# Transposing the experts' rows by small DMAs and 32x32 blocks on VectorE instead of on TensorE

## The chip, the cores and the metric

The kernel runs on one core of a Trainium2 chip. The metric is device time in microseconds of one execution, the median of several runs.

## The reference

Two stages follow each other. A recurrent attention over r, k, v (batch 4, 8 heads, 768 steps, head size 48) gives 3072 rows x of 384 numbers. Each row is then routed to two of eight experts:

```
logits = x @ w_gate;  noisy = logits + log1p(exp(x @ w_noise)) * noise
top2 = the two largest of noisy;  top2_w = softmax over these two
for e in range(8), for k in range(2):
    mask = top2[:, k] == e
    h = maximum(x[mask] @ w1[e], 0)              # 384 -> 1024
    out[mask] += top2_w[mask, k] * (h @ w2[e])   # 1024 -> 384
```

## The kernel before

The attention part and the routing end at about 230 us and are not touched. After them comes a sequence `seq` of chunks (e, ci). Every expert has room for 832 of its rows, held as seven tiles: six of 128 rows and a tail of 64. Expert 0 has three chunks. Experts 1 to 7 have two: chunk (e, 0) holds the tiles 0, 1, 2 (384 rows), chunk (e, 1) the tiles 3, 4, 5 and the tail (448 rows).

Each pass of the loop `for s in range(2, len(seq))` works on one chunk and prepares later ones. Order on every engine is the order in which the program issues instructions; there is no scheduler.

- `xgather` (GpSimd) gathers the rows of the chunk two ahead from `xd` in DRAM, one indirect DMA per tile, into `xg` [128, 392] (384 numbers and 8 gate weights).
- `xT` brings the next chunk's rows into the layout with features on partitions: per tile three TensorE transposes into PSUM (`ptm`, L760), a ScalarE copy to `xh` (L761), a VectorE subtraction for the remainder `xl` (L762; numbers are split into a high and a low part so that three fast matmuls stand for one exact one), and a small copy `GT` of the gate weight (L763). It is a generator: two of its tiles are issued during phase 1, one behind each of the first tiles of phase 2.
- `p1` (phase 1, L781): for eight blocks f of 128 hidden units, nine matmuls into one of three buffers `ph`, then ScalarE's Relu (L783) and VectorE's remainder (L785) into `hb` and, for the tail's 64 columns, `ht`.
- `p2` (phase 2, L815, for the tail L806 and L808): for each tile 24 matmuls (tail: 16) into `pym`, then ScalarE's copy `ot` (L819).
- `emit_out` multiplies by the gate and adds the earlier expert's contribution `pv` (VectorE, L830) and scatters the rows (GpSimd, L834); `pgather` (L742) fetches `pv` for the next expert.
- `w_split` and `wstep` load the next expert's weights: a unit is one DMA of SyncE into one of three staging buffers `stg` (L273), three steps later ScalarE's copy `w0h` or `w1h` (L277), one step later VectorE's remainder (L279). The three units of w1 are taken up in chunk (e, 0), the four of w2 in chunk (e, 1).

Of the kernel before, what the change touches and what calls it, by code (L numbers as in the profile page):

```python
# [9 lines left out]
F32 = mybir.dt.float32  # L10
F32R = mybir.dt.float32r
# [3 lines left out]
AF = mybir.ActivationFunctionType  # L15
# [17 lines left out]
WARM1 = 2  # L33
WARM3 = 1
NLD = 4
XT_AT_0 = 4
XT_AT = 4
LREP = 6
# [4 lines left out]
def kernel(  # L43
# [14 lines left out]
    nc = tc.nc  # L58
    B, H, S, D = r.shape
    N, E = noise.shape  # L60
    DM = H * D
# [4 lines left out]
    ND = DM // 128  # L66
# [3 lines left out]
    NM = 6  # L70
# [3 lines left out]
    WMAX = 3 * 128 + TAIL  # L74
# [4 lines left out]
    NJ = NM + 1  # L79
    XW = DM + E  # L80
# [8 lines left out]
    psum = ctx.enter_context(tc.tile_pool(name="psum", bufs=1, space=bass.MemoryType.PSUM))  # L89
# [3 lines left out]
    moe = stack.enter_context(tc.tile_pool(name="moe", bufs=2, side="left", reuse_waits="tile"))  # L93
# [54 lines left out]
    ident = const.tile([128, 128], F32, name="ident")  # L148
# [33 lines left out]
    for src, store, pw, nm in ((kd[0], kT, pwk, "kT"), (rd[0], rT, pwr, "rT")):  # L182
        pt = psum.tile([128, NP, 128], F32, name="pt0", tag="pa", bufs=3)
# [76 lines left out]
    def w_split(e):  # L260
        W[e] = {}
        units = []

        def unit(mat, c0, c1, src):
            def f():
                if mat not in W[e]:
                    sh = [128, ND, FF] if mat == 0 else [128, NF, DM]
                    W[e][mat] = [wpool[e % 2].tile(sh, F32R, name=f"w{mat}{x}{e % 2}", bufs=1) for x in "hl"]
                hi, lo = (t[:, c0:c1, :] for t in W[e][mat])
                t = stg.tile([128, 1024], F32, name="stg")  # L270
                n = hi.shape[1] * hi.shape[2]
                tv = t[:, :n].rearrange("p (a b) -> p a b", b=hi.shape[2])
                nc.sync.dma_start(tv, src)  # L273
                yield
                yield
                yield
                nc.scalar.activation(hi, tv, AF.Copy)  # L277
                yield
                nc.vector.tensor_sub(lo, tv, hi.bitcast(F32))  # L279
                yield  # L280
            return f()

        for c in range(ND):
            units.append(unit(0, c, c + 1, w1[e, c * 128:(c + 1) * 128, :].rearrange("(c p) f -> p c f", p=128)))
        for c in range(0, NF, 2):
            units.append(unit(1, c, c + 2, w2[e, c * 128:(c + 2) * 128, :].rearrange("(c p) d -> p c d", p=128)))
        return units
# [3 lines left out]
    def wstep():  # L291
        for un in list(wrun):
            if next(un, 0) == 0:
                wrun.remove(un)
        if wq and len(wrun) < 3:
            un = wq.pop(0)
            next(un)
            wrun.append(un)
# [423 lines left out]
    def tw(t):  # L722
        return TAIL if t == NM else 128

    XG, XH, HH, PV, OT, scat_of = {}, {}, {}, {}, {}, {}
    def chunks(e):
        return CHUNKS1 if e else CHUNKS0

    def xgather(e, ci, early_=False):
        for t in chunks(e)[ci]:  # L730
            n = tw(t)
            xg = moe.tile([128, XW], F32, name="xg", bufs=6)
            nc.gpsimd.indirect_dma_start(  # L733
                out=xg[:n], out_offset=None, in_=xd[:GROUPS[GEARLY - 1][1] * 128] if early_ else xd,
                in_offset=bass.IndirectOffsetOnAxis(ap=GR[:n, e * NJ + t:e * NJ + t + 1], axis=0))
            XG[e, t] = xg

    def pgather(e):
        for t in range(NM + 1):
# [4 lines left out]
                in_offset=bass.IndirectOffsetOnAxis(ap=GA[:n, e * NJ + t:e * NJ + t + 1], axis=0))  # L744
            PV[e, t] = pv

    def xT(e, ci):
        xh = moe.tile([128, ND, WMAX], F32R, name="xh")
        xl = moe.tile([128, ND, WMAX], F32R, name="xl")
        XH[e, ci] = (xh, xl)  # L750
        o = 0
        for t in chunks(e)[ci]:
            n = tw(t)
            if (e, t) == (0, NM):
                pt = psum.tile([128, ND, 128], F32, name="ptm", tag=f"py{np2[0] % 2}")
                np2[0] += 1
            else:
                pt = psum.tile([128, ND, 128], F32, name="ptm", tag="pt", bufs=2)
            for d in range(ND):
                nc.tensor.transpose(pt[:, d, :n], XG[e, t][:n, d * 128:(d + 1) * 128], ident[:n, :n])  # L760
            nc.scalar.activation(xh[:, :, o:o + n], pt[:, :, :n], AF.Copy)  # L761
            nc.vector.tensor_sub(xl[:, :, o:o + n], pt[:, :, :n], xh[:, :, o:o + n].bitcast(F32))  # L762
            nc.scalar.activation(GT[:n, e * NJ + t:e * NJ + t + 1], XG[e, t][:n, DM + e:DM + e + 1], AF.Copy)  # L763
            o += n
            yield

    def p1(e, ci):
        w_ = sum(tw(t) for t in chunks(e)[ci])
        xh, xl = XH[e, ci]
        wh, wl = W[e][0]  # L770
        wb = w_ // 128 * 128
        hb = moe.tile([128, NF, 2, 3 * 128], F32R, name="hb", bufs=1)
        ht = moe.tile([128, NF, 2, TAIL], F32R, name="ht", bufs=1) if w_ > wb else None
        HH[e, ci] = (hb, ht)
        parts = [(hb[:, :, :, :wb], 0, wb)] + ([(ht, wb, w_)] if w_ > wb else [])
        for f in range(NF):
            fs = slice(f * 128, (f + 1) * 128)
            ph = psum.tile([128, WMAX], F32, name="ph", tag="pa", bufs=3)
            q = [(a, x, d) for d in range(ND) for a, x in ((wh, xh), (wh, xl), (wl, xh))]
            for j, (a, x, d) in enumerate(q):  # L780
                nc.tensor.matmul(ph[:, :w_], a[:, d, fs], x[:, d, :w_], start=(j == 0), stop=(j == len(q) - 1))  # L781
            for h_, a, b in parts:
                nc.scalar.activation(h_[:, f, 0, :], ph[:, a:b], AF.Relu)  # L783
            for h_, a, b in parts:
                nc.vector.scalar_tensor_tensor(h_[:, f, 1, :], ph[:, a:b], 0.0, h_[:, f, 0, :].bitcast(F32),  # L785
                                               op0=ALU.max, op1=ALU.subtract)
            yield

    np2 = [0]

    def p2(e, ci):
        hb, ht = HH[e, ci]
        wh, wl = W[e][1]
        offs = {t: 128 * j for j, t in enumerate(chunks(e)[ci])}

        ts = chunks(e)[ci]
        for t in ts if (e, ci) != seq[-1] else ts[-1:] + ts[:-1]:
            n, o = tw(t), offs[t]
            py = psum.tile([128, DM], F32, name="pym", tag=f"py{np2[0] % 2}")
            np2[0] += 1  # L800
            ot = moe.tile([128, DM], F32, name="ot", bufs=NOT)
            OT[e, t] = ot
            hs = slice(o, o + n)
            if n == 64:
                for f in range(NF):
                    nc.tensor.matmul(py, ht[:, f].rearrange("p a b -> p (a b)"), wh[:, f, :], start=(f == 0), stop=(f == NF - 1),  # L806
                                     skip_group_check=True)
                    nc.tensor.matmul(py[:n], ht[:, f, 0, :], wl[:, f, :], start=False, stop=(f == NF - 1),  # L808
                                     skip_group_check=True)
                nc.scalar.activation(ot[:n], py[64:], AF.Copy)  # L810
                nc.vector.tensor_add(ot[:n], py[:n], ot[:n])
            else:
                q = [(a, x, f) for f in range(NF) for a, x in ((0, wh), (0, wl), (1, wh))]
                for j, (a, x, f) in enumerate(q):
                    nc.tensor.matmul(py, hb[:, f, a, hs], x[:, f, :], start=(j == 0), stop=(j == len(q) - 1))  # L815
                if (e, ci) == seq[-1]:
                    OT[e, t] = py
                else:
                    nc.scalar.activation(ot, py, AF.Copy)  # L819
            yield t  # L820
# [158 lines left out]
    for s in range(2, len(seq)):  # L979
        e, ci = seq[s]  # L980
        end = s + 1 == len(seq)
        if e and ci == 0:
            nxt = w_split(e + 1) if e + 1 < E else []
            wq.extend(nxt[:ND])
        elif e:
            wq.extend(nxt[ND:])
        xt = xT(*seq[s + 1]) if not end else iter(())
        for j, _ in enumerate(p1(e, ci)):
            while hold:
                emit_out(*hold.pop(0))  # L990
            if XT_AT <= j < XT_AT + 2:
                next(xt, None)
            wstep()
        if s + 2 < len(seq):
            xgather(*seq[s + 2])

        for t in p2(e, ci):
            next(xt, None)
            wstep()
            hold.append((e, t))  # L1000
            while len(hold) > (0 if end else 1):
                emit_out(*hold.pop(0))
        if ci == len(chunks(e)) - 1 and not end:
            while hold:
                emit_out(*hold.pop(0))
            pgather(e + 1)
# [77 lines left out]
```

## Time and profile before

| | us |
|---|---|
| median of 3 runs | 679.81 (676.81 to 680.94) |
| the profiled execution, its own time | 673.61 |
| its span in the trace | 671.8 |
| TensorE busy | 633.3 |
| VectorE busy | 344.7 |
| ScalarE busy | 278.2 |
| GpSimd busy | 251.6 |
| mean granted TensorE clock | 0.968 of full speed |

The busy times are those of one execution, taken by the hardware profiler. In the rows of the profile, PE is TensorE, PEld its weight loads, DVE VectorE, ACT ScalarE, POOL GpSimd, and SPq the queue of SyncE, which issues DMAs. A row of the timeline has start and length in us, engine, line, operation, tile written and tiles read, shape, count, and in brackets the idle time before it and who ended it. A row of the table of groups ends with busy time, mean ns of one, and idle time before.

### The profile page before, as it was taken

What the parts mean: (1) busy time and instruction counts of PE and PEld (TensorE: products, weight loads), DVE (VectorE), ACT (ScalarE), POOL (GpSimd) and SP (SyncE); (2) the same over time, 40 slices, a digit from 0 to 9 for tenths busy, and PEclk for the clock granted to TensorE, in tenths of its full rate; (3) what the DMA queues carried; (4) which work ended last, traced back from release to release, by engine and by line L of the source; (5) the groups of instructions that cost most, each with busy time, mean ns of one, the idle gap of its engine ahead of it and who ended that gap; (6) DMA issues with size and microseconds to landing.
All of it is one profiled execution on the core that took longest, in us unless ns stands there. A gap on an engine that the chain in (4) does not pass through costs nothing.

```text
span 671.8 us, 11840 instructions
## 1 busy us (share of the span) xinstructions
PE 633.3 (94%) x4420; PEld 605.5 (90%) x4421; DVE 344.7 (51%) x837; ACT 278.2 (41%) x809; POOL 251.6 (37%) x318
## 2 busy tenths in 40 slices
PE   7998789897999799999999999999999999999993
PEld 4998788887889799999999999999999999999993
DVE  7675996678547673452525425344362534424230
ACT  4897556655332253252423414244242524422220
POOL 7465323524120353621741442264154236315111
PEclk9999888978699999999999999999999999999997
DMA  7999445734120572532524254262424426302001
GB/s 126 211 220 224 121 115 132 186 86 112 60 91 1 166 251 71 172 119 89 172 86 145 67 164 140 68 184 71 148 89 131 139 68 184 101 27 84 36 4 35
DMA packets 111445, 78.87 MB, mean 117 GB/s; under 512 B 86721, under 2 KB 101441, under 8 KB 111378
## 3 DMA queue, kind: packets, MB, share of 16 engines
q1 hardware_dynamic: 101442, 49.19, 28.5%
q0 software_dynamic: 9936, 28.83, 13.5%
q8 instruction: 37, 0.61, 0.4%
q14 instruction: 30, 0.25, 0.1%
HBM read 59.03 MB, written 19.76 MB: 117 GB/s over the span
## 4 chain that ended last, share of the span: by engine, by line
PE 68%; DVE 2%; ACT 0%; issue 0%; POOL 0%; POOLq 0%
PE ph L781 31%; PE pym L815 30%; PE ptm L760 3%; PE pym L808 2%; PE pym L806 2%; DVE r_oa L579 0%; DVE xl L762 0%; DVE hb L785 0%; PE py L388 0%; PE pl L418 0%; DVE r_ob L586 0%; DVE r_ob L582 0%; ACT xh L761 0%; POOL out_dram L834 0%; PE py L380 0%
## 5 line engine op out<-in xcount | busy, mean ns | idle before, releaser
L815 PE MATMUL pym<-w1h,hb 128*128 128x384 f32 x768 | 204.2, 339 | 0.0
L781 PE MATMUL ph<-xh,w0h 128*128 128x384 f32 (+3 forms) x408 | 141.6, 347 | 1.2 <-ACT xh L761 1.2
L815 PEld LDWEIGHTS pym<-w1h,hb 128*128 128x128 f32 x768 | 139.5, 188 | 0.6
L781 PE MATMUL ph<-xl,w0h 128*128 128x384 f32 (+3 forms) x408 | 138.8, 340 | 0.3 <-DVE xl L762 0.2
L781 PE MATMUL ph<-xh,w0l 128*128 128x384 f32 (+3 forms) x408 | 138.8, 340 | 0.0
L834 POOL DMA_INDIRECT out_dram<-ot,TK x56 | 57.1, 1020 | 216.1 <-DVE ot L830 198.1
L815 PE MATMUL pym<-w1l,hb 128*128 128x384 f32 x384 | 129.2, 336 | 0.0
L785 DVE SCALAR_TENSOR_TENSOR hb<-ph,hb 128x384 fp32r<-128x384 f32 (+1 forms) x136 | 72.3, 532 | 110.2 <-ACT ht L783 70.3
L783 ACT ACTIVATE hb<-ph 128x384 fp32r<-128x384 f32 (+1 forms) x136 | 64.2, 472 | 113.7 <-PE ph L781 111.7
L819 ACT ACTIVATE ot<-pym 128x384 f32<-128x384 f32 x45 | 22.1, 491 | 160.5 <-PE pym L815 160.5
L733 POOL DMA_INDIRECT xg<-xd,GR x56 | 55.1, 984 | 76.7 <-DVE ti L614 37.3
L781 PEld LDWEIGHTS ph<-xh,w0h 128*128 128x128 f32 x408 | 76.7, 188 | 4.1 <-ACT xh L761 1.5
L781 PEld LDWEIGHTS ph<-xl,w0h 128*128 128x128 f32 x408 | 76.7, 188 | 3.2 <-DVE xl L762 0.8
L781 PEld LDWEIGHTS ph<-xh,w0l 128*128 128x128 f32 x408 | 76.6, 188 | 2.6
L815 PEld LDWEIGHTS pym<-w1l,hb 128*128 128x128 f32 x384 | 72.2, 188 | 0.1
L762 DVE TENSOR_TENSOR xl<-ptm,xh 128x384 fp32r<-128x384 f32 (+1 forms) x56 | 29.0, 524 | 81.3 <-ACT xh L761 81.3
L388 PE MATMUL py<-vt,am 128*128 128x96 f32 x384 | 63.3, 296 | 5.6 <-DVE am L346 5.2
L742 POOL DMA_INDIRECT pv<-out_dram,GA x49 | 55.7, 1138 | 28.2 <-issue 13.7
L388 PEld LDWEIGHTS py<-vt,am 128*128 128x128 f32 x384 | 55.8, 211 | 6.5 <-DVE am L346 6.4
L304 POOL TENSOR_TENSOR kd<-kt,tabk 128x384 f32<-128x384 f32 x23 | 24.9, 1083 | 86.0 <-PE pwarm L356 72.5
L319 ACT ACTIVATE cv<-vt,c 128x48 f32<-128x48 f32 x192 | 45.9, 321 | 5.0 <-DVE c L316 4.7
L346 DVE TENSOR_TENSOR am<-pa,mneg 128x512 int32<-128x512 int32 x48 | 30.9, 684 | 15.8 <-PE pa L338 15.8
(196 smaller groups left out, 868.9 us busy)
## 6 DMA issues: line engine op xcount, KB each, us to landing
stg<-in_moe_w_dram SPq DMA_DIRECT2D x24, 512.0 KB, 4.2
stg<-in_moe_w_dram SPq DMA_DIRECT2D x32, 384.0 KB, 3.6
rd<-in_r_dram SPq DMA_DIRECT2D x24, 192.0 KB, 3.9
vt<-in_v_dram SPq DMA_DIRECT2D x24, 192.0 KB, 3.7
xd<-x SPq DMA_DIRECT2D x24, 192.0 KB, 2.3
out_dram<-zrow SPq DMA_DIRECT2D x16, 288.0 KB, 3.6
kt<-in_k_dram SPq DMA_DIRECT2D x23, 192.0 KB, 3.8
xg<-xd,GR POOLq DMA_INDIRECT x56, 3.2
```

The costliest lines, as they stand in the source:

```text
L304: (eng or nc.gpsimd).tensor_mul(kd[i % 3][:, :, :D], kt[i], tabk[:, :, :D])
L319: nc.scalar.activation(cv[:, h, :], vt[i][:, h, :], AF.Copy, scale=c8[:, h, :])
L346: nc.vector.tensor_tensor(am[:, s].bitcast(I32), pa[s].bitcast(I32), mneg.to_broadcast([128, NP, 128]), op=ALU.bitwise_and)
L388: nc.tensor.matmul(o2, AM[i][:, s, p, :], vt[i][:, h, None, :].to_broadcast([128, 2, D]), start=not c and h == 0, stop=h == H - 1, skip_gr ...
L733: nc.gpsimd.indirect_dma_start(out=xg[:n], out_offset=None, in_=xd[:GROUPS[GEARLY - 1][1] * 128] if early_ else xd, in_offset=bass.Indirec ...
L742: nc.gpsimd.indirect_dma_start(out=pv[:n], out_offset=None, in_=out, in_offset=bass.IndirectOffsetOnAxis(ap=GA[:n, e * NJ + t:e * NJ + t + ...
L762: nc.vector.tensor_sub(xl[:, :, o:o + n], pt[:, :, :n], xh[:, :, o:o + n].bitcast(F32))
L781: nc.tensor.matmul(ph[:, :w_], a[:, d, fs], x[:, d, :w_], start=(j == 0), stop=(j == len(q) - 1))
L783: nc.scalar.activation(h_[:, f, 0, :], ph[:, a:b], AF.Relu)
L785: nc.vector.scalar_tensor_tensor(h_[:, f, 1, :], ph[:, a:b], 0.0, h_[:, f, 0, :].bitcast(F32), op0=ALU.max, op1=ALU.subtract)
L815: nc.tensor.matmul(py, hb[:, f, a, hs], x[:, f, :], start=(j == 0), stop=(j == len(q) - 1))
L834: st = nc.gpsimd.indirect_dma_start(out=out, out_offset=bass.IndirectOffsetOnAxis(ap=TK[:n, q:q + 1], axis=0), in_=ot[:n], in_offset=None, ...
```

## The change

For experts 2 to 7 (`ESP = 2`) the rows are gathered into one buffer `xgt` with place for a chunk's four tiles. At the start of the pass for chunk s, `spread` issues 16 SyncE DMAs that copy the rows of chunk s+1 inside SBUF to `xq`: 32 rows and 96 features each, so that every 32x32 block lies on the right partitions. In phase 2 of that pass, one VectorE instruction per tile transposes all blocks of the tile in place, and `xh` and `xl` are made from `xq`. Both `xgt` and `xq` have one buffer. Partition 32a + j now holds feature 96a + 32c + j for c = 0, 1, 2, so w1 of these experts is loaded with its rows in the same order, in four DMAs of 32 rows for each of its three parts. `xh` and `xl` have a new layout for all experts, [128, 14, 3, 32] instead of [128, 3, 448], and phase 1 reads them in runs of 32 columns. The gate copies move to the end of the pass before.

The diff, cut to its core:

```diff
+ESP = 2
...
-                nc.sync.dma_start(tv, src)
+                if mat or e < ESP:
+                    nc.sync.dma_start(tv, src)
+                else:
+                    for a in range(4):
+                        nc.sync.dma_start(tv[32 * a:32 * a + 32, 0, :], src[a])
...
-            units.append(unit(0, c, c + 1, w1[e, c * 128:(c + 1) * 128, :].rearrange("(c p) f -> p c f", p=128)))
+            units.append(unit(0, c, c + 1, w1[e].rearrange("(a c j) f -> c a j f", a=4, j=32)[c] if e >= ESP else
+                              w1[e, c * 128:(c + 1) * 128, :].rearrange("(c p) f -> p c f", p=128)))
...
     def xgather(e, ci, early_=False):
-        for t in chunks(e)[ci]:
+        if e >= ESP:
+            XGT[e, ci] = late[0].tile([128, 4, XW], F32, name="xgt", bufs=1)
+        for j, t in enumerate(chunks(e)[ci]):
             n = tw(t)
-            xg = moe.tile([128, XW], F32, name="xg", bufs=6)
+            xg = XGT[e, ci][:, j] if e >= ESP else moe.tile([128, XW], F32, name="xg", bufs=6)
...
+    def spread(e, ci):
+
+        xq = late[0].tile([128, WMAX // 32, 96], F32, name="xq", bufs=1)
+        XQ[e, ci] = xq
+        w_ = sum(tw(t) for t in chunks(e)[ci]) // 32
+        for q in range(4):
+            m = (w_ - q + 3) // 4
+            for a in range(4):
+                nc.sync.dma_start(xq[32 * a:32 * a + 32, q:w_:4],
+                                  XGT[e, ci][32 * q:32 * q + 32, :m, a * 96:(a + 1) * 96])
+
+    def gate(e, ci, t):
+        q, n = e * NJ + t, tw(t)
+        nc.scalar.activation(GT[:n, q:q + 1], XG[e, t][:n, DM + e:DM + e + 1], AF.Copy)
...
+            if e >= ESP:
+                v = XQ[e, ci][:, g].rearrange("p t (c j) -> p t c j", j=32)
+                nc.vector.transpose(v, v)
...
-            nc.scalar.activation(xh[:, :, o:o + n], pt[:, :, :n], AF.Copy)
-            nc.vector.tensor_sub(xl[:, :, o:o + n], pt[:, :, :n], xh[:, :, o:o + n].bitcast(F32))
-            nc.scalar.activation(GT[:n, e * NJ + t:e * NJ + t + 1], XG[e, t][:n, DM + e:DM + e + 1], AF.Copy)
+            nc.scalar.activation(xh[:, g], v, AF.Copy)
+            nc.vector.tensor_sub(xl[:, g], v, xh[:, g].bitcast(F32))
+            if e < ESP:
+                gate(e, ci, t)
...
-                nc.tensor.matmul(ph[:, :w_], a[:, d, fs], x[:, d, :w_], start=(j == 0), stop=(j == len(q) - 1))
+                nc.tensor.matmul(ph[:, :w_], a[:, d, fs], x[:, :w_ // 32, d], start=(j == 0), stop=(j == len(q) - 1))
...
         xt = xT(*seq[s + 1]) if not end else iter(())
+        sp = not end and seq[s + 1][0] >= ESP
+        if sp:
+            spread(*seq[s + 1])
         for j, _ in enumerate(p1(e, ci)):
             while hold:
                 emit_out(*hold.pop(0))
-            if XT_AT <= j < XT_AT + 2:
+            if XT_AT <= j < XT_AT + 2 and not sp:
                 next(xt, None)
             wstep()
         if s + 2 < len(seq):
             xgather(*seq[s + 2])
 
-        for t in p2(e, ci):
+        for j, t in enumerate(p2(e, ci)):
             next(xt, None)
+            if sp and j == 0:
+                next(xt, None)
             wstep()
...
+        if s + 2 < len(seq) and seq[s + 2][0] >= ESP:
+            for t in chunks(e)[seq[s + 2][1]]:
+                gate(*seq[s + 2], t)
```

The first place is ScalarE in the pass for chunk (4, 0), from the first tile of phase 2 to the first Relu of chunk (4, 1). In the kernel before, the last two of the four copies `xh` of chunk (4, 1) stand here, each behind the `ot` of a tile of phase 2:

```order
L819 ACTIVATE ot_5257<-pym_5256 128x384
L761 ACTIVATE xh_5193<-ptm_5283 128x3x128
L763 ACTIVATE GT_207<-xg_4975 128x1
L819 ACTIVATE ot_5291<-pym_5290 128x384
L761 ACTIVATE xh_5193<-ptm_5317 128x3x64
L763 ACTIVATE GT_207<-xg_4977 64x1
L819 ACTIVATE ot_5330<-pym_5329 128x384
L783 ACTIVATE hb_5361<-ph_5363 128x384
```

In the changed kernel, at the same place, lines are numbered anew (L852 is `ot`, L793 `xh`, L770 the gate copy, L816 the Relu):

```order
L852 ACTIVATE ot_5315<-pym_5314 128x384
L793 ACTIVATE xh_5341<-xq_5173 128x384 x2
L852 ACTIVATE ot_5350<-pym_5349 128x384
L793 ACTIVATE xh_5341<-xq_5173 128x384
L852 ACTIVATE ot_5385<-pym_5384 128x384
L793 ACTIVATE xh_5341<-xq_5173 128x192
L770 ACTIVATE GT_207<-xgt_5310 128x1 x3
L816 ACTIVATE hb_5439<-ph_5441 128x384
```

All four copies are now in phase 2, and the tail's copy (128x192) has moved behind the `ot` of the last tile.

The second place is the DMA queue of SyncE around chunk (4, 1). In the kernel before it holds only weight loads, here w1 and w2 of expert 5 and the first part of w1 of expert 6:

```order
L273 DMA stg_5138<-in_moe_w1_dram 128x1024
L273 DMA stg_5152<-in_moe_w1_dram 128x1024
L273 DMA stg_5166<-in_moe_w1_dram 128x1024
L273 DMA stg_5384<-in_moe_w2_dram 128x2x384
L273 DMA stg_5400<-in_moe_w2_dram 128x2x384
L273 DMA stg_5416<-in_moe_w2_dram 128x2x384
L273 DMA stg_5481<-in_moe_w2_dram 128x2x384
L273 DMA stg_5679<-in_moe_w1_dram 128x1024
```

In the changed kernel the same loads stand between the copies into `xq`: those for chunk (4, 1) ahead of w1, those for chunk (5, 0) ahead of w2:

```order
L765 DMA xq_5173<-xgt_5016 32x4x96 x8
L765 DMA xq_5173<-xgt_5016 32x3x96 x8
L278 DMA stg_5205<-in_moe_w1_dram 32x1024 x4
L278 DMA stg_5222<-in_moe_w1_dram 32x1024 x4
L278 DMA stg_5239<-in_moe_w1_dram 32x1024 x4
L765 DMA xq_5422<-xgt_5310 32x3x96 x16
L275 DMA stg_5462<-in_moe_w2_dram 128x2x384
L275 DMA stg_5478<-in_moe_w2_dram 128x2x384
L275 DMA stg_5494<-in_moe_w2_dram 128x2x384
L275 DMA stg_5543<-in_moe_w2_dram 128x2x384
```

The loads of w2 have moved behind 16 copies whose first one waits for the buffer `xq`, and a load of w1 has become four.

More of the change, by code (lines that the diff above doesn't have):

```diff
@@ L727, in chunks @@
         return CHUNKS1 if e else CHUNKS0
+    XGT, XQ = {}, {}
     def xgather(e, ci, early_=False):
-        for t in chunks(e)[ci]:
+        if e >= ESP:
+            XGT[e, ci] = late[0].tile([128, 4, XW], F32, name="xgt", bufs=1)
+        for j, t in enumerate(chunks(e)[ci]):
             n = tw(t)
-            xg = moe.tile([128, XW], F32, name="xg", bufs=6)
+            xg = XGT[e, ci][:, j] if e >= ESP else moe.tile([128, XW], F32, name="xg", bufs=6)
             nc.gpsimd.indirect_dma_start(
@@ L745, in pgather @@
             PV[e, t] = pv
+    def spread(e, ci):
[10 more added lines that the diff above has]
+        nc.scalar.activation(GT[:n, q:q + 1], XG[e, t][:n, DM + e:DM + e + 1], AF.Copy)
     def xT(e, ci):
-        xh = moe.tile([128, ND, WMAX], F32R, name="xh")
-        xl = moe.tile([128, ND, WMAX], F32R, name="xl")
+        xh = moe.tile([128, WMAX // 32, ND, 32], F32R, name="xh")
+        xl = moe.tile([128, WMAX // 32, ND, 32], F32R, name="xl")
         XH[e, ci] = (xh, xl)
@@ L753, in xT @@
             n = tw(t)
-            if (e, t) == (0, NM):
-                pt = psum.tile([128, ND, 128], F32, name="ptm", tag=f"py{np2[0] % 2}")
-                np2[0] += 1
-            else:
[L758 to L762, printed above, removed]
-            nc.scalar.activation(GT[:n, e * NJ + t:e * NJ + t + 1], XG[e, t][:n, DM + e:DM + e + 1], AF.Copy)
+            g = slice(o // 32, (o + n) // 32)
+            if e >= ESP:
+                v = XQ[e, ci][:, g].rearrange("p t (c j) -> p t c j", j=32)
+                nc.vector.transpose(v, v)
+            else:
+                if (e, t) == (0, NM):
+                    pt = psum.tile([128, ND, 128], F32, name="ptm", tag=f"py{np2[0] % 2}")
+                    np2[0] += 1
+                else:
+                    pt = psum.tile([128, ND, 128], F32, name="ptm", tag="pt", bufs=2)
+                for d in range(ND):
+                    nc.tensor.transpose(pt[:, d, :n], XG[e, t][:n, d * 128:(d + 1) * 128], ident[:n, :n])
+                v = pt[:, :, :n].rearrange("p c (t i) -> p t c i", i=32)
+            nc.scalar.activation(xh[:, g], v, AF.Copy)
+            nc.vector.tensor_sub(xl[:, g], v, xh[:, g].bitcast(F32))
+            if e < ESP:
+                gate(e, ci, t)
             o += n
```

## The prediction

> **What bounds the kernel now.** I read the page's busy times first, then its chain of work that ended last:
>
> ```profile
> PE 633.3 (94%) x4420; PEld 605.5 (90%) x4421; DVE 344.7 (51%) x837; ACT 278.2 (41%) x809; POOL 251.6 (37%) x318
> ...
> PE 68%; DVE 2%; ACT 0%; issue 0%; POOL 0%; POOLq 0%
> PE ph L781 31%; PE pym L815 30%; PE ptm L760 3%; PE pym L808 2%; PE pym L806 2%; DVE r_oa L579 0%; DVE xl L762 0%; DVE hb L785 0%; PE py L388 0%; PE pl L418 0%; DVE r_ob L586 0%; DVE r_ob L582 0%; ACT xh L761 0%; POOL out_dram L834 0%; PE py L380 0%
> ```
>
> TensorE is busy 94% of the span, and its own queue ends last; the transposes of the experts' rows (`ptm`, L760) have 3% of that chain. Next the same chain in order of time, through chunk (4,0), that is expert 4's first chunk, and the start of (4,1); columns are start, length, engine, tile, line, count:
>
> ```profile
> 431.44 7.87 PE ph L781 x45
> 439.30 0.33 PE ptm L760 x3
> 439.63 1.60 PE ph L781 x9
> ...
> 448.91 0.33 PE ptm L760 x3
> 449.24 4.17 PE pym L815 x24
> 453.40 0.33 PE ptm L760 x3
> 453.73 4.37 PE pym L815 x24
> 458.10 9.10 PE ph L781 x45
> ```
>
> Each tile's three transposes hold TensorE for 0.33 us between matmuls that follow without a gap, and a 64-row tail (the one at 453.40) as long as a full tile. There is no step on another engine in this stretch. The view of one stretch says that the granted clock has nothing to give here (the 1.00 in front of the DMA share):
>
> ```profile
> 450.00:460.00 10.00, 10.00 (x58) 9.54 (x57) 1.82 (x4) 1.33 (x5) 3.53 (x7) 1.00 0.32 103
> ```
>
> **The transposes that go.** Experts 2 to 7 have 7 tiles each: 42 x 0.33 = 13.9 us off the path. Nothing on TensorE replaces them. That is the whole gain.
>
> **What is late next: the last tile of the second chunk.** The first change shown on ScalarE decides this. Before, a chunk's four tiles were transposed during phase 1 and behind the first two tiles of phase 2. Now the fourth one's copy `xh` stands behind `ot` of the third and last tile of phase 2, and that `ot` waits for TensorE to finish the chunk. The next chunk's first matmul reads all 448 columns of `xh`, the second all of `xl`. Today's rows at this place (timeline):
>
> ```profile
> 453.44 0.49 ACT L819 ACTIVATE ot<-pym 128x384 f32<-128x384 f32 x1 [3.53 <-PE pym L815]
> 453.83 0.33 ACT L761 ACTIVATE xh<-ptm 128x192 fp32r<-128x192 f32 x1
> 454.19 0.36 DVE L762 TENSOR_TENSOR xl<-ptm,xh 128x192 fp32r<-128x192 f32 x1 [3.78 <-ACT xh L761]
> 457.94 0.36 PE L781 MATMUL ph<-xh,w0h 128*128 128x448 f32 x1
> 458.13 0.36 PE L781 MATMUL ph<-xl,w0h 128*128 128x448 f32 x1
> 458.13 0.49 ACT L819 ACTIVATE ot<-pym 128x384 f32<-128x384 f32 x1 [3.90 <-PE pym L815]
> ```
>
> How TensorE starts after such a wait is seen once, in expert 0:
>
> ```profile
> 234.76 1.29 DVE L762 TENSOR_TENSOR xl<-ptm,xh 128x384 fp32r<-128x384 f32 x3 [2.37 <-ACT xh L761]
> 235.17 0.34 ACT L761 ACTIVATE xh<-ptm 128x192 fp32r<-128x192 f32 x1
> 235.56 0.19 PEld L781 LDWEIGHTS ph<-xh,w0h 128*128 128x128 f32 x1 [0.90 <-ACT xh L761]
> 236.11 0.41 PE L781 MATMUL ph<-xl,w0h 128*128 128x320 f32 x1
> ```
>
> On the clock of the first fence: `ot` starts at 458.13; the next instruction of ScalarE starts 0.39 later (453.44 to 453.83), at 458.52; the copy of 192 columns takes 0.34, plus 0.03 that I allow for reading SBUF instead of PSUM, and ends at 458.89. `xl` starts 0.03 behind it (454.16 to 454.19), takes 0.36 and ends at 459.28. TensorE follows 0.06 later (236.05 to 236.11), so the second matmul starts at 459.34 instead of 458.13: 1.2 us later, and all matmuls behind it with it. This comes once per expert from 2 to 7: 6 x 1.2 = 7.2 us back. The other boundary, from a second chunk to the next expert, has three tiles to prepare and four tiles of phase 2 to hide them; its last `xh` stands behind the second `ot`, with a 4.2 us tile and the tail still to run, so I charge nothing there. If that cover were gone it would cost the same 1.2 us six more times.
>
> **What VectorE gains in work.** 42 transposes of 128x384 are not in the trace. From below they cost nothing, if they pass while VectorE idles; from above I take 1.25 us, the next larger pass over SBUF:
>
> ```profile
> L279 DVE TENSOR_TENSOR w0l<-stg,w0h 128x1024 fp32r<-128x1024 f32 x24 | 29.8, 1247 | 1.9 <-ACT w0h L277 1.9
> ```
>
> VectorE works 1.82 of 10 us in the stretch quoted above, so even 1.25 us fits into a 4.2 us tile of phase 2, and the fourth tile's transpose waits for no `ot` of the last tile. On the path: 0. The Trainium skill (VectorE: DVE Perf Modes, section on the three transpose paths) gives 311 ns on VectorE against 390 ns on TensorE for 128x128 in bf16 and advises TensorE for a full block; as an estimate, three such blocks are 0.93 us, which would change nothing here, and TensorE's own 0.33 us in this trace is far below what that page charges it.
>
> **What the layout costs.** `xh` and `xl` are now read in runs of 32 columns. The nearest rows read 96 columns, once in two runs of 48 (L388, `vt` repeated) and once in one piece (L380):
>
> ```profile
> L388 PE MATMUL py<-vt,am 128*128 128x96 f32 x384 | 63.3, 296 | 5.6 <-DVE am L346 5.2
> L380 PE MATMUL py<-zb,rT 128*128 128x96 f32 x160 | 33.7, 296 | 0.0
> ```
>
> Both take 296 ns: I take 0, and keep 3% of phase 1's 31% (6 us) as the other end, because the runs are shorter and the type is another.
>
> **What SyncE's queue gains.** A chunk's 16 small copies (L765 of the changed kernel) stand, in the second chunk of an expert, ahead of three w2 loads. The first copy waits for the last `xl` of the running chunk (one buffer `xq`), so until 459.3. Today those loads were issued 16 us earlier, at 442.08. ScalarE reaches the first `w1h` in (4,1) at 465.90, with 1.2 us of boundary at 467.1; its wait holds up the `hb` copies queued behind it, and those hold the three `ph` buffers of TensorE. The rows, from the timeline, the table of DMA issues and the landing time of the issue at 442.08 alone:
>
> ```profile
> 19.28 0.32 SPq L248 DMA_DIRECT2D stg<-in_w_dram  x1
> 128.84 0.36 SPq L398 DMA_DIRECT2D xd<-x  x1
> 129.30 0.39 SPq L122 DMA_DIRECT2D kt<-in_k_dram  x1
> 129.74 0.69 SPq L122 DMA_DIRECT2D rd<-in_r_dram  x1
> 130.53 0.51 SPq L122 DMA_DIRECT2D vt<-in_v_dram  x1
> 442.08 4.03 SPq L273 DMA_DIRECT2D stg<-in_moe_w_dram  x3
> xd<-x SPq DMA_DIRECT2D x24, 192.0 KB, 2.3
> DMA to landing us min/median/max: 3.2/3.2/3.2
> 465.90 0.85 ACT L277 ACTIVATE w1h<-stg 128x768 fp32r<-128x768 f32 x1
> 467.24 0.49 ACT L783 ACTIVATE hb<-ph 128x384 fp32r<-128x384 f32 x1 [0.49 <-PE ph L781]
> 467.87 0.56 DVE L785 SCALAR_TENSOR_TENSOR hb<-ph,hb 128x384 fp32r<-128x384 f32 x1 [1.13 <-ACT ht L783]
> 468.35 0.21 DVE L785 SCALAR_TENSOR_TENSOR ht<-ph,ht 128x64 fp32r<-128x64 f32 x1
> ```
>
> An issue lies between 0.32 us (one row) and 0.79 us (129.74 to 130.53, 1024 pieces). A copy has 96 or 128 pieces, like the 128 rows of `xd`, whose successor starts 0.46 later and the next 0.44: I take 0.44. Sixteen are 7.0 us, to 466.4; the first w2 load lands 3.2 us later, at 469.6. Then `w1h` 0.85, to the VectorE pass of the fifth `hb` 0.63 (467.24 to 467.87), to the end of its `ht` 0.69 (to 468.56): `ph` is free at 471.8. TensorE wants it for its eighth block at 459.34 + 62 x 0.202 (9.10 / 45) = 471.9. So it just fits: each 0.1 us more per issue costs 1.6 us per chunk, from a point that is already reached. Between the ends 0.32 and 0.79, the wait is 0 to 5.5 us per chunk, 0 to 33 us in six chunks (the w2 of experts 2 to 7). I charge 0.2 us per chunk, 1 us in all. That only one DMA holds each of eight semaphores, so that the ninth waits for the first, costs nothing as long as a copy lands within 8 x 0.44 = 3.5 us; `xd` took 2.3.
>
> In an expert's first chunk ScalarE wants the three w1 parts at these times, the boundary being at 431.4:
>
> ```profile
> 438.15 1.05 ACT L277 ACTIVATE w0h<-stg 128x1024 fp32r<-128x1024 f32 x1
> 442.12 1.06 ACT L277 ACTIVATE w0h<-stg 128x1024 fp32r<-128x1024 f32 x1
> ```
>
> The 16 copies start behind the second of four tiles of the previous phase 2, some 5.5 us ahead of the boundary, and end 1.5 us behind it; the 12 pieces of w1 follow at 0.42 each, so the first part is issued by 3.2 us and the last by 6.6, and they land 3.2 us later, at 6.4 and 9.8, against 6.7 and 10.7 wanted. Hidden, just; if a part is 1 us late, TensorE still has two blocks of 1.6 us to run in the other `ph` buffers. The gathers into the single `xgt` now wait for the copies to be read, about 10 us into a chunk of 27; they are wanted a chunk later.
>
> **The sum.** 673.6 us for the profiled execution (span 671.8) - 13.9 + 7.2 + 1 = 667.9, so 5.7 us or 0.8% less. The median of the three runs is 679.8, 6.2 us above the profiled one; the same 5.7 us off gives **674**. I take 1% (6.8 us) as the least that a measurement of this kernel can tell from no change.
>
> **Rivals.**
> 1. The boundary is hidden (ScalarE's queue is not as late as I say, or the gain of the transposes comes free in another way): -13.9 + 0 to 3, so 666 to 669. For it speaks that no wait stands there today; against it the order of ScalarE's rows, with no free engine in between.
> 2. Slower: the queue of SyncE. Place: `w1h` of a second chunk; price: 16 x the excess of an issue over 0.44. At 0.51 us per issue the gain is gone, from 0.58 us it is more than 1% slower; at 0.69, the length of `rd`, 4 us x 6 = 24 us give 697 on the median. For it speak the rows of `rd` and `vt` with their 1024 pieces; against it that a copy has an eighth of them.
> 3. The copies do not overlap: each is paid from issue to landing, one behind the other. 16 x 2.3 = 37 us instead of 7, so each of six chunks ends some 30 us later: +180. The rows at 128.84 to 130.53 speak against it: four issues in 2.1 us while the first alone takes 2.3 to land. The Trainium skill (DMA: Bandwidth & Descriptors, rules for kernel authors) says that transfers under 64 KB pay mostly overhead and that splitting by partitions does not help; these copies have 37 to 49 KB. By that rule the copies are poor, but the trace shows the overhead overlapped.
> 4. The runs of 32 columns cost up to 3% of phase 1: +6 us, which leaves 680, no change.
>
> **Chances.** Forecast with its small wait 0.55 (two thirds of it within 1%, since it lies 1 us from that line); rival 1 0.17, faster; rival 2 0.19, of which a third stays within 1%; rival 3 0.01; rival 4 0.08, within 1% for 0.05 of it and slower where rival 2's wait joins it. Faster by over 1%: 0.35, within 1%: 0.48, slower: 0.17. The range reaches down to rival 1, 665, and up to 0.55 us per issue (0.11 x 16 x 6 = 10.6 us above 673.1), 684, with about one in ten beyond.
>
> **What would show it.** No `ptm` of experts 2 to 7 on TensorE; six idle stretches of about 1 us at `ph` of a second chunk, released by `xh` and `xl`, none at a first chunk; SyncE's 16 copies 0.44 us apart; idle time of ScalarE at `w1h` of 2 to 3 us and almost none of TensorE at the eighth `ph`. I am wrong if TensorE waits there for `hb`, if the `ph` matmuls of 384 columns take more than today's 0.175 us apiece, or if VectorE's transposes wait for the copies in phase 2.

## The result, and the profile after

The changed kernel takes 726.77 us (717.42 to 731.57) against 678.31 us, a ratio of 1.065 [1.060, 1.070]: slower by 48.5 us, where 674 was forecast. The profiled execution took 726.19 us. Medians and ranges here and below hold every run, the ratios leave out one slow run each of the changed kernel (731.57 us) and of experiments 4 (681.74) and 8 (713.52).

The page of the changed kernel, busy times and the chain that ended last:

```profile
span 724.4 us, 11993 instructions
PE 646.9 (89%) x4294; PEld 610.1 (84%) x4295; DVE 364.8 (50%) x879; ACT 279.8 (39%) x809; POOL 248.9 (34%) x318
PE 62%; DVE 11%; issue 9%; SPq 8%; ACT 5%; DMA 3%; POOL 0%; DVEq 0%; POOLq 0%; ACTq 0%
PE pym L848 25%; PE ph L814 15%; SPq L765 8%; PE py L394 6%; DMA stg<-in_moe_w_dram 3%; PE pt L332 3%; PE pa L344 3%; PE py L386 2%; PE pl L424 2%; DVE w0l L284 2%; PE pym L841 1%; PE pym L839 1%; ACT hb L816 1%; ACT w0h L282 1%; PE ptx L412 1%
```

TensorE has 126 instructions fewer (4294 for 4420), the 42 x 3 transposes. But it fills only 89% of the span, and SyncE's queue, which was not on the chain before, has 8% of it: nearly all of that is L765, the copies of `spread`.

Where the time lies shows one stretch in both kernels, from the first matmul of chunk (2,0) to the first of chunk (7,1). A row has the stretch, its length, the busy time of PE, PEld, DVE, ACT and POOL, the granted clock, the DMA share and GB/s. The kernel before:

```profile
316.22:630.61 314.39, 314.39 (x1783) 304.08 (x1783) 130.39 (x247) 112.61 (x279) 123.81 (x155) 1.00 0.36 111
```

The changed kernel:

```profile
323.72:682.94 359.22, 320.65 (x1665) 302.23 (x1665) 148.69 (x285) 114.45 (x280) 120.39 (x153) 0.96 0.43 121
```

The stretch is 44.8 us longer, of the 52.6 us between the two profiled executions. Some 7.5 us lie ahead of it (323.72 for 316.22), and are not the change's: the first experiment, which has no copies, reaches the same place at 323.96. Inside the stretch TensorE never rested before; now it rests for 38.6 us (359.22 - 320.65), and the clock granted to it is 0.96 instead of 1.00.

The same places as in the prediction, chunks (4,0) and (4,1), now at 455.41 to 520.79, by phases:

```profile
455.41:469.56 14.15, 12.81 (x74) 12.49 (x73) 5.61 (x9) 4.26 (x11) 7.07 (x8) 1.00 0.67 163
469.56:486.82 17.26, 13.45 (x73) 12.19 (x72) 7.82 (x14) 6.38 (x14) 7.59 (x9) 1.00 0.45 115
486.82:505.54 18.72, 15.16 (x73) 13.56 (x73) 6.89 (x17) 6.54 (x20) 6.14 (x8) 1.00 0.51 149
505.54:520.79 15.25, 15.25 (x89) 14.94 (x88) 7.41 (x15) 4.16 (x9) 2.28 (x4) 1.00 0.26 73
```

The first three phases have idle time of TensorE, the fourth none. The timelines of the changed kernel say who ends it. First the queue of SyncE, start and length of each group of issues:

```profile
450.17 10.29 SPq L765 DMA_DIRECT2D xq<-xgt  x16
460.50 6.05 SPq L278 DMA_DIRECT2D stg<-in_moe_w_dram  x12
487.19 10.78 SPq L765 DMA_DIRECT2D xq<-xgt  x16
498.01 6.78 SPq L275 DMA_DIRECT2D stg<-in_moe_w_dram  x4
```

Then ScalarE, where a bracket has the wait and what ended it:

```profile
465.80 1.06 ACT L282 ACTIVATE w0h<-stg 128x1024 fp32r<-128x1024 f32 x1 [3.43 <-DMA stg<-in_moe_w_dram]
470.05 1.06 ACT L282 ACTIVATE w0h<-stg 128x1024 fp32r<-128x1024 f32 x1 [2.81 <-DMA stg<-in_moe_w_dram]
473.54 1.06 ACT L282 ACTIVATE w0h<-stg 128x1024 fp32r<-128x1024 f32 x1 [2.06 <-issue]
486.03 0.49 ACT L852 ACTIVATE ot<-pym 128x384 f32<-128x384 f32 x1 [3.26 <-PE pym L848]
486.42 0.35 ACT L793 ACTIVATE xh<-xq 128x192 fp32r<-128x192 f32 x1
501.44 0.84 ACT L282 ACTIVATE w1h<-stg 128x768 fp32r<-128x768 f32 x1 [6.19 <-DMA stg<-in_moe_w_dram]
```

And TensorE, all its rows with a wait there, and the two that stand at the boundary beside one:

```profile
467.88 0.44 PE L814 MATMUL ph<-xh,w0h 128*128 128x384 f32 x1 [1.34 <-DVE hb L818]
475.03 0.44 PE L848 MATMUL pym<-w1h,hb 128*128 128x384 f32 x1 [2.18 <-ACT hb L816]
477.22 0.62 PE L848 MATMUL pym<-w1h,hb 128*128 128x384 f32 x2 [0.80 <-DVE w0l L284]
485.65 0.34 PE L848 MATMUL pym<-w1h,hb 128*128 128x384 f32 x1
486.82 0.47 PE L814 MATMUL ph<-xh,w0h 128*128 128x448 f32 x1 [0.83 <-ACT xh L793]
487.22 0.48 PE L814 MATMUL ph<-xl,w0h 128*128 128x448 f32 x1
503.64 0.44 PE L814 MATMUL ph<-xh,w0h 128*128 128x448 f32 x1 [3.56 <-DVE ht L818]
```

Read backwards, they give the chain. In (4,1) TensorE rests 3.56 us for the remainder `ht`, which is queued behind ScalarE's Relu; the Relu stands behind `w1h`, which waits 6.19 us for a load of w2; and the load stood behind 16 copies, issued in 10.8 us. In (4,0) the same happens with w1: 12 pieces behind 16 copies, three stops of ScalarE at `w0h`, three of TensorE, 1.34 + 2.18 + 0.80 = 4.3 us. With the 0.83 at the boundary the idle time is 8.7 us for the pair of chunks. The seven tiles' transposes give 2.3 us back, and the rest, 65.38 - 57.47 + 2.3 - 8.7 = 1.5 us, lies in matmuls that are slower right behind a wait (0.44 and 0.62 us where 0.34 and 0.51 stand in other rows; 57.47 is the pair before, 431.44 to 488.91).

### The profile page after: what moved, and what is told of

It reads as the page before. It is cut to its first block, busy times and chain, and to the rows that moved or that the text cites. A ratio compares the mean times of both kernels' runs of the same rounds, so it can differ in the third digit from the quotient of the medians.

```text
span 724.4 us, 11993 instructions
## 1 busy us (share of the span) xinstructions
PE 646.9 (89%) x4294; PEld 610.1 (84%) x4295; DVE 364.8 (50%) x879; ACT 279.8 (39%) x809; POOL 248.9 (34%) x318
## 4 chain that ended last, share of the span: by engine, by line
PE 62%; DVE 11%; issue 9%; SPq 8%; ACT 5%; DMA 3%; POOL 0%; DVEq 0%; POOLq 0%; ACTq 0%
PE pym L848 25%; PE ph L814 15%; SPq L765 8%; PE py L394 6%; DMA stg<-in_moe_w_dram 3%; PE pt L332 3%; PE pa L344 3%; PE py L386 2%; PE pl L424 2%; DVE w0l L284 2%; PE pym L841 1%; PE pym L839 1%; ACT hb L816 1%; ACT w0h L282 1%; PE ptx L412 1%
## 5 line engine op out<-in xcount | busy, mean ns | idle before, releaser
L848 PE MATMUL pym<-w1h,hb 128*128 128x384 f32 x768 | 207.3, 346 | 10.3 <-issue 2.6
L814 PE MATMUL ph<-xh,w0h 128*128 128x384 f32 (+3 forms) x408 | 144.6, 355 | 30.9 <-DVE ht L818 15.3
L848 PEld LDWEIGHTS pym<-w1h,hb 128*128 128x128 f32 x768 | 143.4, 194 | 16.2 <-issue 4.3
L814 PE MATMUL ph<-xl,w0h 128*128 128x384 f32 (+3 forms) x408 | 143.1, 351 | 0.3 <-DVE xl L794 0.2
L814 PE MATMUL ph<-xh,w0l 128*128 128x384 f32 (+3 forms) x408 | 142.7, 350 | 0.0
L848 PE MATMUL pym<-w1l,hb 128*128 128x384 f32 x384 | 132.0, 344 | 0.8 <-issue 0.8
L816 ACT ACTIVATE hb<-ph 128x384 fp32r<-128x384 f32 (+1 forms) x136 | 63.2, 469 | 110.1 <-PE ph L814 77.5
L852 ACT ACTIVATE ot<-pym 128x384 f32<-128x384 f32 x45 | 22.1, 491 | 124.7 <-PE pym L848 98.8
L743 POOL DMA_INDIRECT xgt<-xd,GR x42 | 44.3, 1055 | 52.4 <-DMA xq<-xgt 37.2
L752 POOL DMA_INDIRECT pv<-out_dram,GA x49 | 49.5, 1009 | 28.5 <-issue 16.3
L794 DVE TENSOR_TENSOR xl<-xq,xh 128x384 fp32r<-128x384 f32 (+1 forms) x42 | 22.2, 530 | 70.0 <-ACT xh L793 70.0
L282 ACT ACTIVATE w0h<-stg 128x1024 fp32r<-128x1024 f32 x24 | 25.2, 1056 | 42.5 <-DMA stg<-in_moe_w_dram 25.6
```

Source lines behind the costliest of these rows:

```text
L743: nc.gpsimd.indirect_dma_start(out=xg[:n], out_offset=None, in_=xd[:GROUPS[GEARLY - 1][1] * 128] if early_ else xd, in_offset=bass.Indirec ...
L752: nc.gpsimd.indirect_dma_start(out=pv[:n], out_offset=None, in_=out, in_offset=bass.IndirectOffsetOnAxis(ap=GA[:n, e * NJ + t:e * NJ + t + ...
L814: nc.tensor.matmul(ph[:, :w_], a[:, d, fs], x[:, :w_ // 32, d], start=(j == 0), stop=(j == len(q) - 1))
```

## The experiments

Ratios are against the kernel before on the same chip (its median 679.74 us for the first four, 674.94 us for the rest).

**1. The layout alone.** No expert is spread; `xh` and `xl` keep the new layout.

```diff
-ESP = 2
+ESP = 8
```

> ESP = 8: no expert is spread, w1 loads and gathers are those of before, TensorE transposes all tiles; only the layout of xh and xl in 32-column runs stays. Theory Q (SyncE's queue: 16 copies at 0.64 us stand ahead of the weight loads, ScalarE waits for them and TensorE for ScalarE): same as before, ratio 0.995 to 1.005. Rival L (phase 1 reads 32-column runs more slowly, or the copies into the new layout are slower): 1.02 or more of the 1.065, with matmuls of 384 columns further apart than 0.175 us.

Measured: 680.62 us, 1.002 [0.9998, 1.0044]. The group of phase 1's third matmul in this kernel, count, busy time and mean ns of one:

```profile
L814 PE MATMUL ph<-xh,w0l 128*128 128x384 f32 x168 | 56.6, 337 | 0.0
```

In the kernel before:

```profile
L781 PE MATMUL ph<-xh,w0l 128*128 128x384 f32 x168 | 56.5, 337 | 0.0
```

And its stretch from (2,0) to (7,1), as long as before (314.39):

```profile
323.96:638.61 314.65, 314.65 (x1782) 304.24 (x1782) 130.47 (x247) 112.70 (x279) 123.57 (x155) 1.00 0.36 111
```

Runs of 32 columns are read as fast as one piece. The fourth rival is out; what is slow belongs to the copies.

**2. The copies behind the weight loads.** The copies are issued inside phase 1, behind its third block and so behind the loads; nothing else is changed.

```diff
-        if sp:
-            spread(*seq[s + 1])
         for j, _ in enumerate(p1(e, ci)):
...
             wstep()
+            if sp and j == 2:
+                spread(*seq[s + 1])
```

> The changed kernel with one edit: the 16 copies are issued behind the third step of the weight loads in phase 1 instead of ahead of phase 1. Same DMAs, same bytes. Theory Q: ScalarE's waits for w0h and w1h (some 73 us) go, the boundary wait of 1.2 us in six chunks stays, so 13.9 less and 7.2 more than before: ratio 0.99 (0.98 to 1.0). Rival D (the extra DMA traffic and small pieces slow all transfers, wherever they stand): stays above 1.03. Rival L: stays above 1.02.

Measured: 678.39 us, 0.998 [0.995, 1.001]. No wait of ScalarE for w1 is left, and 0.2 us for w2. Moving the same copies a few places along one queue takes back all of the 6.5%. Rival D, the extra traffic itself, is out. The stretch from (2,0) to (7,1):

```profile
319.91:632.73 312.82, 305.39 (x1666) 292.43 (x1665) 149.23 (x285) 116.02 (x280) 123.93 (x153) 1.00 0.48 135
```

The idle time is down from 38.6 to 7.4 us, and the clock is back at 1.00. Of the 7.4 us, six waits at the boundary are 5.1; the other 2.2 stand beside stops of ScalarE, which the last section takes up. They are part of the few microseconds by which I missed 0.99; the rest is not explained.

**3. The tail's tile earlier.** The last two tiles are both prepared ahead of the last tile of phase 2, the copies stay ahead of the loads.

```diff
-            if sp and j == 0:
+            if sp and j < 2:
                 next(xt, None)
```

> The changed kernel with one edit: the fourth tile of a second chunk is prepared behind the second tile of phase 2 instead of the third. Theory Q: the six waits of 1.2 us for xh at a second chunk go, and the copies of the next chunk, which wait for that tile's xl, start some 3.5 us earlier, so that ScalarE's waits for w1h shrink from 5.6 us to about 3, those for w0h stay: ratio 1.03 to 1.045. If the queue were not the cause, only the 7.2 us would go: 1.055.

Measured: 704.86 us, 1.036 [1.032, 1.040], as expected. The gain of 0.029, some 20 us, is more than six waits of 1.2 us: the last `xl` is what frees `xq`, so with it the copies, and behind them the loads, also start earlier. The waits that remain are those of the queue:

```profile
ACT w0h L282 <- DMA stg<-in_moe_w_dram: 25.3, 10, 4.9
ACT w1h L282 <- DMA stg<-in_moe_w_dram: 23.3, 6, 4.9
```

(Columns: total us, times, longest.) In the changed kernel they are 25.6 and 30.1. A wait for `w1h` is now 3.9 us on average, where I had expected about 3.

**4. Both edits.**

> Both edits together: copies behind the weight loads, fourth tile one step earlier. Theory Q: nothing of the change stays on TensorE's path but the 13.9 us that it takes away: ratio 0.98 (0.975 to 0.985). Rivals D and L: above 1.0.

Measured: 667.92 us, 0.982 [0.978, 0.986]: faster than both kernels, by 11.8 us than the one before. The stretch from (2,0) to (7,1):

```profile
321.01:623.47 302.46, 301.76 (x1665) 293.04 (x1665) 149.92 (x286) 115.76 (x279) 127.32 (x152) 1.00 0.50 139
```

It has the same TensorE instructions as the changed kernel, no idle time to speak of (0.7 us), and the clock at 1.00. So 301.76 us is what this work takes, and the changed kernel's stretch is 314.39 - 12.6 (transposes) + 38.6 (idle) + 18.9 (the same matmuls slower, 320.65 - 301.76) = 359.2 us. This sum closes by construction; what checks it is that the 12.6 lies near the 12.9 that 39 tiles at 0.33 us give. Between experiments 2 and 4 lie 10.4 us in this stretch, 312.8 to 302.5: 6.7 us of idle time (4.5 at the boundaries, 2.2 beside stops of ScalarE) and 3.6 us by which the same matmuls are shorter.

**5. What one copy costs the queue.** Both edits of experiment 4, and in the last chunk, where no copies or loads are left, 12 more DMAs into buffers that nothing else uses then: two each of six shapes.

```diff
...
+        for _ in range(2):
+            nc.sync.dma_start(three(at(32, 288)), src[32:64, :3, 96:192])
+        for _ in range(2):
+            nc.sync.dma_start(at(32, 288), src[32:64, 0, :288])
+        for _ in range(2):
+            nc.sync.dma_start(at(32, 96), src[32:64, 0, 96:192])
+        for _ in range(2):
+            nc.sync.dma_start(three(at(128, 288)), src[:, :3, 96:192])
+        for _ in range(2):
+            nc.sync.dma_start(three(at(32, 288)), xd[0:96, 96:192].rearrange("(a p) f -> p a f", p=32))
+        for _ in range(2):
+            nc.sync.dma_start(at(128, 96), src[:, 0, 96:192])
...
```

> The kernel with both edits, and in the last chunk, where SyncE has nothing left to issue, twelve more DMAs that nothing reads, two of each shape: the copy as it is (32 partitions x 3 tiles x 96), the same bytes in one run per partition (32x288), a third of them (32x96), 128 partitions x 3 x 96, the first shape read from DRAM, and 128x96. The question is why a copy holds SyncE for 0.60 us and not 0.36. Theory N (number of pieces, as the prediction had it): 32x288 and 32x96 with 32 pieces fall to 0.32 to 0.36 us, 128x3x96 with 384 pieces goes to 1 us or more. Rival S (source and target both in SBUF): all shapes stay near 0.6 us but the one from DRAM, which falls to about 0.4. Rival P (only 32 partitions): the two shapes with 128 partitions fall below 0.4, the others stay.

Measured, in the order of the diff, ns of one issue (least, median, most):

```profile
L783 SPq DMA_DIRECT2D xh<-xgt x2: 585/592/598, 601.5 to 602.2; - x2
L785 SPq DMA_DIRECT2D xh<-xgt x2: 589/592/594, 602.8 to 603.4; - x2
L787 SPq DMA_DIRECT2D xh<-xgt x2: 588/592/595, 604.1 to 604.7; - x2
L789 SPq DMA_DIRECT2D xl<-xgt x2: 641/670/698, 605.4 to 606.1; - x2
L791 SPq DMA_DIRECT2D xl<-xd x2: 437/526/615, 606.8 to 607.4; - x2
L793 SPq DMA_DIRECT2D xl<-xgt x2: 494/546/599, 607.9 to 608.5; - x2
```

The first three shapes, of 96, 32 and 32 pieces and 36, 36 and 12 KB, take 0.59 us alike, and the fourth, with 384 pieces and 144 KB, only 0.67; 128 pieces of the last one take 0.49 and 0.60. The number of pieces, from which I had taken my price, sets almost nothing here. Nor do the 32 partitions: the two shapes with 128 do not fall below 0.4. That a source in DRAM is cheaper has one row for it (437) and one against (615). The kind of memory alone can't be the answer either: in the kernel before, two loads of one shape from one line, both from DRAM, differ by almost a factor of two in their medians:

```profile
L122 SPq DMA_DIRECT2D vt<-in_v_dram x24: 368/700/3218, 3.8 to 163.2; - x24
L122 SPq DMA_DIRECT2D kt<-in_k_dram x23: 384/386/812, 4.3 to 161.9; - x23
```

So the price of a copy is measured, and what sets it stays open. The run took 657.07 us, one run.

**6. and 7. One place each.** The copies stand behind the loads in one kind of chunk alone: behind w1 in first chunks (6), behind w2 in second chunks (7). The diff of 6; that of 7 has the other number:

```diff
-        if sp:
+        if sp and ci != 0:
             spread(*seq[s + 1])
...
             wstep()
+            if sp and ci == 0 and j == 2:
+                spread(*seq[s + 1])
```

> The changed kernel, with the copies behind the weight loads only in an expert's first chunk (ahead of w1 no more, still ahead of w2). Theory Q: the waits for w0h go, some 30 us by the lengths of chunks (2,0) to (6,0), those for w1h stay: ratio 1.02 (1.01 to 1.03). Rival (one of the two places makes the whole loss): 1.065 or 0.998.

> The complement: the copies behind the weight loads only in second chunks (ahead of w2 no more, still ahead of w1). Theory Q: the waits for w1h go, some 21 us by the lengths of chunks (1,1) to (6,1), those for w0h stay: ratio 1.035 (1.025 to 1.045). The two gains together should give the 1.065 - 0.998 of both places.

Measured: 689.33 us, 1.023 [1.020, 1.027], and 695.07 us, 1.033 [1.028, 1.038]; both as expected. The waits of 6:

```profile
ACT w1h L282 <- DMA stg<-in_moe_w_dram: 31.4, 8, 6.5
PE ph L814 <- DVE ht L818: 16.2, 5, 3.8
```

The waits of 7:

```profile
ACT w0h L282 <- DMA stg<-in_moe_w_dram: 39.6, 15, 5.0
PE ph L814 <- DVE hb L818: 6.9, 5, 2.9
```

Each edit takes away the wait at its own place and leaves the other. Taken off experiment 2, the place of w2 costs 1.023 - 0.998 = 2.5%, 17 us, and that of w1 1.033 - 0.998 = 3.5%, 24 us. Counted from the changed kernel instead, the two gains are 1.065 - 1.023 = 4.2% and 1.065 - 1.033 = 3.2%, together 7.4%, where both edits at once gained 6.7%.

**8. The pieces of w1 alone.** No copies (`ESP = 8`), but the w1 of experts 2 to 7 in four DMAs of 32 rows per part.

```diff
-ESP = 2
+ESP = 8
...
-                if mat or e < ESP:
+                if mat or e < 2:
...
-            units.append(unit(0, c, c + 1, w1[e].rearrange("(a c j) f -> c a j f", a=4, j=32)[c] if e >= ESP else
+            units.append(unit(0, c, c + 1, w1[e].rearrange("(c a j) f -> c a j f", a=4, j=32)[c] if e >= 2 else
```

> ESP = 8 (new layout alone, all transposes on TensorE), and each w1 unit of experts 2 to 7 loaded by four DMAs of 32 rows instead of one of 128, with its rows in the order of before. Theory Q: the loads go out when a staging buffer falls free, more than 10 us ahead of their use, and 12 issues of 0.46 us do not matter there: ratio 0.995 to 1.008, and landing up to 5.6 us. Rival P1 (pieces of 32 rows are slow in themselves and hold up ScalarE): 1.015 or more.

Measured: 675.06 us, 1.001 [0.999, 1.003]. An issue of a piece takes what it takes in the changed kernel (median 419 ns):

```profile
L278 SPq DMA_DIRECT2D stg<-in_moe_w_dram x72: 310/419/1556, 240.4 to 536.9; - x72
```

They land after 2.8 us in the median and 7.4 at most, where I had expected 5.6 at most. At the old place of the loads the pieces cost nothing. What they add to the loss when they stand behind the copies, no run tells apart.

## Why the prediction was wrong

By place, the 44.8 us of the stretch are -12.6 (transposes) + 5.0 (six waits at the boundary) + 15.3 (five waits in second chunks, behind w2) + 18.2 (the rest of the 38.6, all of it waits in first chunks, behind w1) + 18.9 (slower matmuls). The forecast had 7.2 for the boundary, 1 for w2 and nothing for the last two.

**The step that failed is the price of a copy on SyncE's queue.** It said 0.44 us, from the row of `xd` and the number of pieces. The copies in the changed kernel, ns of one:

```profile
L765 SPq DMA_DIRECT2D xq<-xgt x192: 589/597/2015, 289.2 to 661.8; - x192
```

With the 0.04 us between two, sixteen take 10.3 us instead of 7.0. The bounds I had kept, 0.32 and 0.79, held it, but the range that I gave stopped at 0.55. I chose by a likeness (pieces) that experiment 5 refutes: no row of before had a copy inside SBUF, and `rd`, 0.69 long and 0.79 from the next start, was as near as `xd`.

**The second rival's mechanism holds at w2, with its formula.** 10.3 - 7.0 + 0.2 = 3.5 us per second chunk is what it gives at 0.64 us; the row at 503.64 has 3.56, the longest of the five such waits in the stretch, which are 3.1 us on average. With 3.5 us six times, this place alone would have made 694 us.

**"Hidden, just" at w1 fell with the same number.** The copies started 5.24 us ahead of the boundary (450.17 to 455.41; 5.5 said), but ended 5.1 us behind it instead of 1.5. The first part then came at 465.80, 10.4 us behind the boundary, where 6.7 was wanted. I had priced this place at nothing although less than 1 us was in hand (6.4 against 6.7, 9.8 against 10.7), and had not made it a rival; it is the dearer of the two (18.2 us of idle time against 15.3; 24 us against 17 by experiments 6 and 7). A second error is smaller: I let every load land 3.2 us after its issue. The chain has the last piece of the second part, from its issue to its landing:

```profile
464.27 5.61 DMA stg<-in_moe_w_dram
```

GpSimd's `pv` gathers run beside it (the first starts at 463.36); that they slow it is likely and not shown. Experiment 8, without copies, has landings of up to 7.4 us as well.

**What slow matmuls add was not in the sum.** 18.9 us of the loss is the same matmuls at a lower clock or just after a wait. One such place, TensorE in chunk (3,0):

```profile
406.88 0.34 PE L848 MATMUL pym<-w1h,hb 128*128 128x384 f32 x1
409.66 0.68 PE L848 MATMUL pym<-w1h,hb 128*128 128x384 f32 x1 [2.44 <-ACT w0h L282]
410.14 0.52 PE L848 MATMUL pym<-w1l,hb 128*128 128x384 f32 x1
```

And the stretch around it:

```profile
403.90:422.00 18.10, 14.62 (x74) 13.37 (x72) 7.80 (x13) 6.36 (x14) 5.75 (x8) 0.91 0.39 105
```

After 2.44 us without a matmul one takes twice its time, and the granted clock of the 18 us is 0.91. Here the wait is paid a second time. That the waits bring the clock down is read from such rows and from the 1.00 of experiments 2 and 4, where they are gone; how the 18.9 us divide between the clock and the first matmuls behind a wait, no run tells.

The Trainium skill (TensorE: Matmul & The Clock Gate, section "Why this matters for your kernels") asks for no gap over about 3 us between bursts, since the clock then falls to half; here the row at 409.66 has it after 2.44 us, and the wait of 3.56 us at 503.64 was in a stretch whose clock stayed at 1.00, so the gap's length alone does not decide it in this trace. Behind waits of 2.35 and 2.44 us the first matmul took 0.69 and 0.68 us, behind the five waits of 2.85 to 3.56 us in second chunks 0.44 to 0.46.

**What was right.** The transposes: 12.6 us of TensorE's time are gone in the stretch (39 of the 42 tiles, 12.9 by 0.33). The boundary: the second matmul of (4,1) starts at 487.22, and would have at 485.65 + 2 x 0.175 = 486.0, so 1.2 us as worked out, with `xh` behind `ot` as the cause (486.03, 486.42). The layout is free. VectorE's transposes take this, and no row of TensorE waits for them:

```profile
L783 DVE STREAM_TRANSPOSE xq<-xq x42: 369/570/575, 309.6 to 679.9; 128x384 f32<-128x384 f32 x36, 128x192 f32<-128x192 f32 x6
```

The third rival, copies paid from issue to landing one by one, is out: they are issued 0.64 us apart and land in 2.0 (experiment 5's median). Of the ways to be wrong that I named, TensorE waiting for `hb` came true, with the tail's part `ht` as the one that came last.

## What to carry to other kernels

Small DMAs that only prepare the next stage belong behind the loads that the running stage needs, on a queue that works in order: with the 16 copies ahead of the loads this kernel became 6.5% slower, with the same copies behind them it stayed within 0.5% of before, and with the tail's tile moved too it became 1.8% faster. Where a sum has a point "already reached", its slope times the whole spread of the unknown price is the forecast's true uncertainty, and a place that is "hidden, just" by the same price must be moved along with it. Before pricing a new kind of transfer from a row, look whether any row moves data between the same kinds of memory; where none does, as here, a likeness is no reason to narrow the bounds.

## What the runs showed of the hardware

A copy inside SBUF held SyncE's queue for 0.59 us whether it had 32 pieces or more (192 copies of 96 or 128 pieces, four samples of 32), while loads from DRAM took 0.42 (32 rows, L278) and 0.37 (128 rows, the kernel before's median).

ScalarE stops for 2.4 to 5.4 us at a time in experiment 2, and for 1.6 to 4.7 us in experiment 4, where the profile finds nothing on the core that ended the wait ("remote"). The waits of experiment 2:

```profile
ACT ot L852 <- remote: 18.6, 4, 5.4
ACT hb L816 <- remote: 16.9, 5, 4.5
```

One of them, in its timeline:

```profile
511.34 0.49 ACT L852 ACTIVATE ot<-pym 128x384 f32<-128x384 f32 x1 [4.76 <-remote]
```

In the DMA view of 508 to 511.4 us, the queue of instructions has a packet while the gathers fill the engines:

```profile
q0 software_dynamic: 208, 0.63, 63.8%
...
q8 instruction: 1, 0.02, 1.8%
```

For this stop, a wait of ScalarE for its own instructions behind the gathers would fit. But in four other stops of experiment 2 (331.5 to 335.8, 336.3 to 341, 453.6 to 457.4 and 563.5 to 568.9 us) that queue has no packet. Nor do the copies explain the stops: experiment 1, which has none, shows three (of up to 3.4 us), and experiment 5, with all copies, none; it ran on another chip. Their cause stays open, with the 4 us by which experiment 2's stretch (312.8 us) is longer than 314.4 - 12.9 + 7.2 = 308.7. Of these, 2.2 us are waits of TensorE beside such stops.
